# A fused attention and bilinear-FFN kernel whose whole order is written out as a table: one table of order, engines and PSUM banks is replaced by another

## The chip, the cores and the metric

The kernel runs on one core of a Trainium2 chip. The metric is device time in microseconds, the median of the timed runs. The kernel before takes 294.14 us (three runs: 294.15, 293.53, 294.14).

## The reference

Inputs are float32. Attention works in chunks of 64 tokens, each chunk for itself; its output goes through a bilinear feed-forward network.

```python
# q, k, v: (B=8, H=8, S=576, D=64);  w_a, w_b: (512, 1536);  w_out: (1536, 512)
scores = scale * q_c @ k_c.T              # per chunk of 64 tokens and head
attn   = exp(scores - max);  attn /= attn.sum(-1) + 1e-9
x      = (attn @ v_c) as (4608 tokens, 512)
a, b   = x @ w_a, x @ w_b
out    = ((a * b) @ w_out).astype(float32)    # (4608, 512)
```

## The kernel before, in words

**Tiling.** The 4608 tokens are nine blocks (K) of 512 tokens, and eighteen units (u) of 256 tokens; two units make a block. For each unit the kernel loads q, k and v (float32, by head), casts them to bf16 (`f32` to `qkb` and `vb`), transposes q and k into `qkT` (on TensorE for the first four units, `turn_pair`; with a transposing DMA from the SP queue after that, `turn_dma`), and then runs three short TensorE stages, called slots: scores into PSUM and exp on ScalarE into `E`; row sums through a matmul with `ones`, whose inverse is made by Ln and Exp(-x) on ScalarE (`inv`); values, multiplied by `inv` on VectorE into `xT`. These slots use 64x64 tiles of the array, all other matmuls the whole of it.

**FFN.** Block 0 is done plainly (`ffn`, L772): for each of twelve groups `ft` of 128 columns of the hidden layer one product with `WB` and one with `WA` (four matmuls of 512 columns each; for the first four groups each product is cut in two halves, so that it can start on half of the input), a copy of the first out of PSUM (`bsb`) and a multiplication (`AB`). From block 1 on the products are done by a seven-product scheme (`side_group`, L861; output: `out_seven`, L1166; last output block: `out_last`, L1004) on sums and differences of inputs (`x_sums`, `SX`), of weights (`side_sums`, `weight_sums`) and of `AB` (`out_sums`), made on VectorE or GpSimd. Each product is 4 or 6 matmuls of 256 columns; partial results are copied out of PSUM between products that share a bank (`keep_copy`).

**Loads.** Weights come as float32 in pieces of 512 KB into a ring of eight buffers (`wst`): `load_four` for WB and WA, `load_wo` for WO; each is cast to bf16 by one of GpSimd, ScalarE and VectorE. Nearly all loads and stores go through the SP queue, in the order of the table.

**Order.** Nothing is scheduled at run time. Every piece of work is an operation with a number, recorded by `Planner.op` with its dependencies. `Planner.follow` then reads the table `ORDER_OF_ALL`. A word is a letter for the engine that runs it (a TensorE, b ScalarE, c VectorE, d GpSimd, e the SP queue), the operation's number, and for an operation that takes PSUM banks their numbers. So `a49:0` is operation 49 on TensorE in bank 0, and `c50` is operation 50 on VectorE. `f0` is a fill: a matmul of zeros into bank 0, 512 columns wide, whose result nobody reads (L1474). Operations without a choice of engine keep theirs; casts, copies and sums may stand under one of two or three engines.

```python
for word in table.split():
    if word[0] == "f":
        order.append(fill(int(word[1:])))       # a matmul of zeros
        continue
    name, _, banks = word[1:].partition(":")
    o, e = self.ops[int(name)], self.ENGINES[word[0]]
    assert e in o["engs"] and o["deps"] <= done
```

**A wait that the table makes.** When an operation of VectorE that reads and writes SBUF alone (`fast`) stands in the table, the next GpSimd operation in the table gets a dependency on it.

**Operations that the text below names.** 48, 51, 57, 60, 66, 69, 75, 78: casts of the first block's q and k. 84, 85: casts of its v. 94, 95: reciprocals of row sums (VectorE). 13, 15, 17, 19: casts of the first pieces of WB and WA. 91, 92, 97, 98: the first four multiplications into `xT`. 32, 34 (loads) and 33, 35 (casts): the last pieces of WA. 118, 119, 137, 138 (loads) and 132, 151 (casts): v of units 2 and 3. 208, 227; 220, 271; 224, 275: the scores, sums and values slots of units 2 and 3. 225, 226, 276, 277: their multiplications into `xT`. 287, 289, 351: first products of block 1. 268, 269 (casts), 270 (transposing DMA) and 308 (scores): unit 5.

Of the kernel before, what the change touches and what calls it, by code (L numbers as in the profile page):

```python
# [97 lines left out]
a341:6 c207 a336 b337 d251 d255 d257 d286 e44 e38 a338 b339 d39 e263 b45 c199 a331:7 c332 c203 a342 a340:3  # L98
b343 a382:5 a351:1 a345 c344 e42 e262 e40 d41 b346 c347 a349:7 b350 a353 b354 a362:2 c363 a355 a359 c360 a357
c358 b43 a364:0 a372:2 b352 c365 a369 d268 e46 c230 a367 b47 c238 c242 a411:6 b370 a376 c377 c378 b368 a373  # L100
d231 d243 c356 e265 e264 b269 a412 b374 a371:3 c375 a384 b413 b385 c233 c232 c239 c241 c234 c244 c240 e214
b383 e213 b218 a423:0 a390 a424 c391 e211 e212 b217 d335 a388 c389 a393:4 a380:7 b381 a426 a427 e216 b428 a400
a398 a431 a395:2 a386 b401 a432 a407 c237 e266 e267 b279 c236 a429:3 d235 c425 b433 c394 c387 e270 b399
a308:04 b310 c396 b408 b309 a404 a430 a443 a320:12 b405 b321 a416 b322 d366 c348 a444 a414 c245 c361 c259 c261
c397 c434 c379 c453 a324:40 c445 e219 a280:12 b323 c325 a446 a447 c326 c448 a402:6 c406 b281 b282 a300:41 b302
b301 b303 e215 d278 a304:20 d435 c392 e292 e312 e291 a403:3 c409 d410 a418 c419 d457 c305 c306 a535:1 a420
c421 c436 c438 b415 b297 a526:4 a587:6 a536 a441:7 b442 a439:2 b440 a519:0 c520 d437 a524 b525 c417 e293 e294
d298 a517:3 a522 b523 c518 a531 b532 a527:0 c533 b537 a528 b529 c530 e311 a561:5 b562 b317 a579:3 a540 a544
a538 c545 c580 a584 c539 a542 c543 c541 e449 e314 e313 b318 a559:0 d422 d463 d521 b585 a577:3 a591 d459 c461
b560 c578 a582 b583 b592 c593 a597:2 c598 d454 d462 d534 d458 a612:4 a586:7 a588 b589 c590 d594 a595:3 b596  # L110
a605 c606 a599 c600 a619 e315 a601 a603 c604 c602 d456 d464 e465 e296 e467 a617 a614:6 a547:0 a548 b618 d455
b620 e316 b327 e299 a328:75 a623 a626 b330 b329 c615 a550 b627 e472 e319 a488:65 b489 b490 e466 c613 c624
a480:47 b482 c549 a638 c639 a640 c641 a551 c552 e295 d546 a622:0 b481 b483 a506:65 a510:37 b508 d307 a484:42
a555 c628 d616 e493 c486 c485 a621:5 c625 c629 c460 b507 e451 e498 e496 e468 a553:2 e494 e469 e452 e501 e471
b509 c512 c511 c630 c631 a753:6 a644 a693:4 a556 b557 e470 a636:7 a642 c643 e495 b477 e492 c645 d575 a554
a634:3 b637 a563 c632 d607 e474 a698 a564 b699 c635 a696 b565 c694 c558 c697 a691:5 a705 d646 c581 c692 d573
c574 a700:0 a701:4 a702 a566 a733:1 b706 c707 b478 b703 a712 e491 e450 b503 e497 b504 a567 c704 e500 a735:5
d633 a718 a716 b713 d608 e475 e476 e502 e473 c568 b487 a709:2 a760:3 c736 a758 c754 c719 b759 a710 b711 d647
d648 d650 a751:6 d609 c717 a714 c734 a756 c752 b757 c715 c720 a761:4 a765 b766 c767 a769:0 a762 a721:6 a771:7
a722 c763 a773 c764 a777 e499 e652 c723 d610 e651 e479 b772 b657 a779 a775 b774 c778 a793 b770 a791 e505  # L120
a668:61 d755 c780 c794 b670 a514:34 a724 a725 a800 b516 b515 a660:14 d768 d708 d611 c649 c792 c776 d781 c695
b669 a680:36 b681 b661 b682 b662 c726 e571 a788:5 c789 a797 b801 a786:3 a729 c787 c798 d513 a664:15 a684:64
b683 c685 c686 a730 b663 a814 a796:3 a812 a795:6 a727:4 a728 e572 e656 e672 e671 b677 c665 c666 a810:1 a825:5
d804 c805 e674 b731 b813 e673 e653 b678 c802 b811 a808:0 a818 c799 d576 d803 a737 a832 a738 a816 e654 b658
c809 c826 c790 c819 d782 c815 c817 c820 c806 a902:5 a830 e570 b739 e655 b833 a827:3 c828 a834:2 a835:7 b831
a836 b837 c732 a839 c840 c841 e676 e675 b687 a900:6 c838 d807 a846 a740 d749 c747 d748 b903 a925:3 a852 c853
a850 c851 a932 b901 a930 c926 c933 d667 d784 b931 b847 a741 c742 a848 c849 a936 a934:7 b937 c938 e679 a865:23
b870 e659 e858 a688:04 b689 b690 a947 c783 d829 c948 a939 e855 a927:1 c928 c940 a935:3 c941 a864:04 d750 b869
a892:62 b896 b895 a951 a943:1 c952 e885 e884 e882 c944 b867 b866 b868 a945:2 a843:6 c946 a949 c950 a844 a953
c954 b845 a962:4 d821 d889 c963 c822 a970:7 a967 c968 a891:05 a914:34 c929 b897 c917 c823 d942 e886 c916 c893  # L130
c978 a965 b966 a874 a875 b876 e887 b920 e856 a960:4 a974 e883 b888 c975 c976 c894 d842 c961 e857 b862 a969:3
a871:0 a872 a879 a971 b972 c973 a984:5 a880 a992 a986 c985 d955 d854 d979 a877:4 a1006 a878 c987 e569 e745
c873 b861 e860 d980 a990 e859 e1059 c993 c991 e746 c1007 a982:1 b983 d981 d898 a1074:0 c824 a1001:7 c1002
a1004 a988 a999:3 c1000 b881 d785 a904 a1008:7 b1005 a1010 a905 a1009:3 b1011 c956 e744 a1013 b1014 c899 a907
a1020 a908 d964 c989 c977 c994 c995 d957 a1103:2 c1012 a1024 d996 b1021 c1015 a1026 c1075 c1104 b906 a1076:1
b1077 d921 c1025 a1108 a1105:6 b1109 a1110 c1027 b1111 c909 a1022 c1023 e890 a1039:27 b1044 c1106 e1030 e1031
e743 e863 a915:34 b918 b1043 b919 a1114 c1115 a1112:5 c1116 a1117 c1118 a1121:7 a1066:63 b1070 b1069 c1122
a1038:24 b1040 a1125 c1126 b1041 b1042 a1129 e1029 e1034 d998 e1032 c1130 e1056 d923 d922 d1003 a1138:3 c1139
e1057 e1058 e1060 c1036 a1127 a1113:6 c1128 a1092:20 b1035 c1016 a1065:45 c1067 a1017:3 a1143 a1123:1 a1018
a1045:4 c1119 b1071 c1095 c1124 c1094 d1062 b1019 b1144 a1131 a1140:0 e912 c1132 a1149 a1046 c1150 e1033 e910  # L140
e1210 e1061 e1235 b1072 e1209 a1048 a1049 b1050 e913 a1147:2 a1145 b1146 c1068 a1164 c1047 c1141 d959 d958
d1156 d997 a1053 e1208 c1157 e1212 c1107 c1159 c1158 c1120 b1063 a1054 b1055 c1165 a1152 b1153 a1148:6 c1154
a1160:5 a1051:4 a1162:0 c1151 b1161 d1028 d924 a1170 c1171 a1168 c1169 a1179:7 a1182 a1078 a1079 a1177:6 a1052
b1163 c1183 a1252:2 a1184 b1185 c1180 c1133 d1142 c1178 d1181 d1155 a1188 c1189 a1186:7 b1080 a1187:6 a1166
a1277:3 a1191 c1073 a1081 a1082 d1136 c1190 c1167 d1172 d1175 b1253 a1254:1 a1202 d1099 d1134 c1192 c1193
a1204 a1200 d1194 e1037 e1064 d1100 b1255 a1282 c1203 b1283 c1278 c1083 c1205 a1198 b1199 c1201 a1284 c1285
a1288 b1289 a1286:7 c1290 a1217:34 a1093:56 b1096 b1221 a1279:0 c1280 b1222 a1291 b1292 a1295:5 a1299 d1206
# [1378 lines left out]
```

## Time and profile before

| | |
|---|---|
| Median of the timed runs | 294.14 us |
| Span of the profiled execution | 291.4 us |
| Median less span | 2.7 us |
| TensorE (PE) busy | 285.0 us, 98% of the span, 3522 matmuls |
| VectorE (DVE) busy | 245.6 us, 84% |
| ScalarE (ACT) busy | 181.5 us, 62% |
| GpSimd (POOL) busy | 175.3 us, 60% |
| HBM | 37.75 MB read, 9.44 MB written |

The profile gives the profiled execution's span, from its first instruction to its last, and no other time of that execution; the row below the span is the distance to the median. PE is the matmuls, PEld the loads of stationary operands, SPq the SP queue's own instructions. A matmul's length in the profile runs to its modelled end, and the next one starts before that: the distance between the starts is what a matmul costs TensorE.

### The profile page before, as it was taken

To read this page: it belongs to the slowest core of one execution; us is meant where nothing else is said; L and a number is where in the kernel's file an instruction comes from. 1 tells how busy PE (TensorE), PEld (TensorE's weight loads), DVE (VectorE), ACT (ScalarE), POOL (GpSimd) and SP (SyncE) were. 2 spreads that over 40 slices of the span, in tenths; PEclk is the share of its full clock that TensorE was granted. 3 is DMA by queue.
4 is the path that set the end of the run, shared out by engine and by line. 5 is a ranking of instruction groups with operands and counts; after the bars stand their busy time and mean duration, and the time that the engine had idled before them with its cause. 6 is when DMAs were issued, how large, how long until landed. Compare 5 with 4: busy or idle time off the path is not lost.

```text
span 291.4 us, 8635 instructions
## 1 busy us (share of the span) xinstructions
PE 285.0 (98%) x3522; PEld 232.6 (80%) x3522; DVE 245.6 (84%) x432; ACT 181.5 (62%) x308; POOL 175.3 (60%) x168
## 2 busy tenths in 40 slices
PE   8999989999999999999999999999999999999995
PEld 3545448887888888888888888888888888888884
DVE  2758989999897999989998989888997788697893
ACT  1767878978877775795675468525944684333221
POOL 3354248443789389835739694569447764676540
PEclk9999999999999999999999999999999999999999
DMA  7999999999998789939996995939290210003034
GB/s 244 335 395 393 310 282 340 246 216 246 213 213 219 191 175 274 240 75 201 260 259 158 203 277 126 253 88 242 76 219 3 80 69 2 0 2 144 3 133 156
DMA packets 140248, 55.09 MB, mean 189 GB/s; under 512 B 126256, under 2 KB 131504, under 8 KB 140208
## 3 DMA queue, kind: packets, MB, share of 16 engines
q1 hardware_dynamic: 138976, 53.43, 71.8%
q10 hardware_dynamic: 1232, 1.11, 1.1%
q8 instruction: 27, 0.44, 0.7%
q14 instruction: 13, 0.11, 0.1%
HBM read 37.75 MB, written 9.44 MB: 162 GB/s over the span
## 4 chain that ended last, share of the span: by engine, by line
PE 91%; ACT 3%; DVE 2%; DMA 1%; issue 1%; POOL 0%; SPq 0%; POOLq 0%
PE F L861 49%; PE F L1166 24%; PE F L772 6%; PE F L1004 3%; PE F L1474 2%; PE F L635 1%; PE F L645 1%; PE F L492 1%; PE F L673 1%; DMA f<-in_k_dram 1%; ACT inv L697 1%; ACT inv L695 1%; DVE xT L722 0%; POOL wst L821 0%; ACT E L528 0%
## 5 line engine op out<-in xcount | busy, mean ns | idle before, releaser
L326 ACT COPY part<-F 128x512 f32<-128x512 f32 x87 | 50.4, 591 | 49.0 <-PE F L861 32.2
L895 POOL TENSOR_TENSOR AB<-AB,bsb 128x512 bf16<-128x512 bf16 x45 | 51.7, 1156 | 38.7 <-DVE wst L1123 15.5
L899 DVE TENSOR_TENSOR bsb<-F,part 128x512 bf16<-128x512 f32 x72 | 49.0, 685 | 10.4 <-PE F L861 4.9
L326 ACT COPY wst<-F 128x512 f32<-128x512 f32 (+1 forms) x43 | 24.0, 561 | 30.5 <-PE F L861 14.7
L861 PEld LDWEIGHTS <-WB 128*128 128x128 bf16 x384 | 37.3, 98 | 5.2 <-issue 0.5
L861 PEld LDWEIGHTS <-WA 128*128 128x128 bf16 x384 | 37.2, 98 | 4.8 <-issue 0.3
L899 DVE TENSOR_TENSOR AB<-F,part 128x512 bf16<-128x512 f32 x48 | 32.9, 686 | 3.7 <-PE F L861 1.6
L1123 POOL TENSOR_TENSOR wst<-AB 128x512 bf16<-128x512 bf16 x27 | 31.0, 1155 | 7.0 <-PE F L1166 4.7
L861 PEld LDWEIGHTS <-Ta 128*128 128x128 bf16 x288 | 27.9, 98 | 3.9 <-issue 0.5
L861 PEld LDWEIGHTS <-Tb 128*128 128x128 bf16 x288 | 27.4, 98 | 4.4 <-issue 0.9
L1166 PEld LDWEIGHTS <-AB 128*128 128x128 bf16 x288 | 28.0, 98 | 3.4
L1166 PEld LDWEIGHTS <-wst 128*128 128x128 bf16 x288 | 27.8, 98 | 3.4
L861 PE MATMUL F<-wst,Ta 128*128 128x256 bf16 x192 | 28.8, 273 | 0.1
L861 PE MATMUL F<-wst,Tb 128*128 128x256 bf16 x192 | 28.8, 273 | 0.0
L861 PE MATMUL F<-wst,WB 128*128 128x256 bf16 x192 | 28.8, 273 | 0.0
L861 PE MATMUL F<-wst,WA 128*128 128x256 bf16 x192 | 28.8, 273 | 0.0
L861 PE MATMUL F<-xT,WA 128*128 128x256 bf16 x192 | 28.2, 273 | 0.0
L861 PE MATMUL F<-xT,WB 128*128 128x256 bf16 x192 | 28.1, 273 | 0.0
L1166 PE MATMUL F<-WO,AB 128*128 128x256 bf16 x192 | 25.5, 273 | 0.0
L326 DVE COPY part<-F 128x512 f32<-128x512 f32 x33 | 22.4, 684 | 2.7 <-PE F L861 2.0
L326 ACT CAST qkb<-f 128x1024 bf16<-128x1024 f32 (+1 forms) x24 | 23.2, 986 | 0.3 <-DMA f<-in_q_dram 0.3
L1123 POOL TENSOR_TENSOR wst<-wst,AB 128x512 bf16<-128x512 bf16 x16 | 18.4, 1155 | 6.0 <-DVE wst L1123 5.9
(126 smaller groups left out, 551.7 us busy)
## 6 DMA issues: line engine op xcount, KB each, us to landing
f<-in_q_dram SPq DMA_DIRECT2D x32, 256.0 KB, 4.2
f<-in_v_dram SPq DMA_DIRECT2D x32, 256.0 KB, 4.2
f<-in_k_dram SPq DMA_DIRECT2D x28, 256.0 KB, 4.8
out_dram<-osb SPq DMA_DIRECT2D x28, 256.0 KB, 3.5
wst<-in_moe_w_b_dram SPq DMA_DIRECT2D x6, 512.0 KB, 7.8
wst<-in_moe_w_a_dram SPq DMA_DIRECT2D x6, 512.0 KB, 6.9
wst<-in_moe_w_out_dram SPq DMA_DIRECT2D x6, 512.0 KB, 6.8
out_dram<-osb SPq DMA_DIRECT2D x12, 128.0 KB, 2.4
```

The lines of the kernel that those rows point to most:

```text
L326: return A.copy(out=out, in_=in_) if e == "act" else ENG[e].tensor_copy(out=out, in_=in_)
L492: T.transpose(turned()[:, r, :], qkb[hu][:, x, mm * 512 + r * 128:mm * 512 + r * 128 + 128], identity)
L635: T.matmul(PS[j][cl * 64:cl * 64 + 64, c:c + 64], chunk_of(u, 1, m, j, 2 * g + cl), chunk_of(u, 0, m, j, 2 * g + cl), start=True, stop=True,)
L645: T.matmul(SU[cl][j * 64:j * 64 + 64, :], ones[cl * 64:cl * 64 + 64, :], E[u % 2][cl * 64:cl * 64 + 64, j, :], start=True, stop=True,)
L772: T.matmul(f_of(b)[:, 0:n].rearrange("p (u t) -> p u t", u=len(us)), w[ft][:, kt, :], x[:, us[0]:us[-1] + 1, kt, :], start=(kt == 0), stop ...
L861: T.matmul(f_of(bank)[:, q * 256:q * 256 + 256], lhs(2 * g + q, kt), rhs[:, kt, :], start=(first and q == 0 and kt == 0), stop=(q == 1 and ...
L895: op(("dve", "pool"), TIMES, lambda e: ENG[e].tensor_tensor(out=dst, in0=dst, in1=b, op=MULT), r=bk, w=key, prio=-300, fast=True)
L899: op("dve", c_dve(512), lambda e: V.tensor_tensor(out=dst, in0=two(f_of(bank)), in1=two(pab[s][i]), op=ADD), r=[("ps", id(bank)), ("part", ...
L1004: T.matmul(f_of(bank)[:, 0:256], lhs[:, i, h], rhs[:, i, :], start=(first and i == 0), stop=(i == NP - 1), skip_group_check=True)
L1123: op(*long_op(hs), lambda e, i=i, x=x, y=y, o_=o_: ENG[e].tensor_tensor(out=SS[i][:, s], in0=x[:, s], in1=y[:, s], op=o_), r=fts + [(name, ...
L1166: T.matmul(f_of(bank)[:, at:at + 256], lhs[:, i, tt * 128:tt * 128 + 128], rhs[:, i, :], start=(first and at == 0 and i == 0), stop=(i == ...
L1474: "fn": lambda e: T.matmul(F[at], zero[:, 0:128], zero, start=True, stop=True),
```

## The change

`ORDER_OF_ALL` is another table over the same 1675 operations; nothing else differs. No operation is added or dropped. Of the fills 22 are left of 30. Engine changes: 51 operations go from VectorE to GpSimd and 46 the other way, 43 from ScalarE to VectorE and 40 the other way, 11 from ScalarE to GpSimd and 10 the other way. TensorE has the same 578 operations in another order and in other banks; the SP queue has the same DMAs in another order.

Lines of the table that the text below speaks of (before is -, after is +):

```diff
-c113 e0 b1 e2 b3 e4 e8 b5 e6 e9 c48 f0 f1 f2 f3 f4 f5 f6 f7 f0 f1 a49:0 c50 d51 f2 a52:1 d57 f3 f4 a58:2 b7
-d60 e10 e11 f5 a61:3 d66 b62 c53 a54:45 c59 f6 f7 a63:67 e12 b55 b56 a67:0 c68 b64 b65 f1 f2 a93:12 d69 a70:3
-b71 f4 f5 f6 a72:45 c94 b73 a86:67 b74 b75 b88 d78 a79:0 b80 f3 f3 f4 a76:3 b77 f5 f1 f4 f5 a81:45 a99:17 b87
-c84 c95 d85 a96:03 c97 f6 a90:62 b89 c91 d13 e16 d17 e135 e14 d15 c98 e18 e134 e20 e22 b83 b101 b82 f5 a106:50
...
-b128 a204:4 e136 e24 d148 a149:6 b150 c122 c25 c258 e26 c27 c252 c247 c254 c256 b206 b202 a196:7 a208:03 b210
-b209 e137 a227:12 b228 b229 a181:6 c183 c198 a192:4 b194 a185:5 c187 e138 e32 a220:30 a271:12 a177:4 e34 d33
-c35 c179 a189:6 c191 d249 e119 e118 c132 a193:7 a205:5 c260 b222 d253 b151 a224:04 b221 b223 c225 c226 d285
-b273 b272 b274 a275:36 c276 e36 b37 a201:2 a197:1 c277 c283 c284 c195 a287:0 b288 a289:4 b290 a333:3 c334
...
+c113 e0 b1 d48 f0 f0 f0 f0 f0 f0 f0 a49:0 c50 e2 b3 e4 b5 d51 d57 a52:1 c53 f2 a58:2 e6 b7 d60 c59 f3 a61:3 b62 e9 b69
+f4 f4 f4 a63:45 b65 e11 a54:67 e8 c75 f0 a76:0 c78 c77 f1 a79:1 b64 a93:23 a70:5 c95 b55 b66 b56 b80 a86:46 b88 b87
+d84 c71 c94 a67:0 a81:71 b83 b82 a106:64 b68 b108 b107 f1 f1 a72:17 e10 d85 f3 f3 f3 f3 f3 a90:30 b74 b89 a110:54
+a96:67 c98 e12 c13 e16 d17 e14 d15 b73 a99:12 b100 c91 c97 a103:71 c92 a152:3 b109 c111 b101 c112 b102 c104 a164:2
...
+b120 a121:4 c150 b147 b131 a189:2 b122 a208:03 b194 e32 a227:64 a196:7 b210 b209 c183 a220:13 b228 b229 a177:0 d33 e34
+c260 c258 c191 c198 d35 a197:2 c253 a271:64 c179 d255 a193:7 a205:0 b221 b222 b223 b273 e137 c187 e138 d151 b272 c199
+e118 e119 c132 a224:13 c195 c226 c225 d285 a275:52 e36 e44 e265 e263 b274 c277 c276 c283 c284 a201:4 b37 c257 a351:6
...
```

More of the change, by code (lines that the diff above doesn't have):

```diff
@@ new lines @@
+a1267:06 b1387 e1263 a1374 e1264 d1276 d1368 c1379 d1355 d1380 b1270 b1386 a1435 b1436 a1437:4 c1441 a1446:3 b1447
+b1271 a1450 c1375 c1451 a1442 a1454 c1455 a1468 a1400:07 b1403 d1432 a1381:26 b1384 c1443 c1275 a1438:1 c1444 d1347
+d1348 b1469 a1463:4 a1448:0 c1464 a1465:6 c1449 c1466 d1445 d1467 b1383 a1474 b1475 b1404 a1456 a1452 c1453 c1457
+b1385 a1369:4 c1458 a1489 b1490 a1399:26 a1421:75 c1402 b1405 c1422 a1370 b1371 c1423 a1470 b1471 a1472:1 a1388:3
+a1477 b1478 d1350 a1473:6 a1389 c1476 a1493 c1479 a1391 c1401 a1487:7 a1485:5 d1483 c1488 a1491 c1492 a1392 c1480
@@ new lines @@
+d1519 b1581 a1602 d1579 a1597:5 b1583 c1600 c1598 a1520:2 b1603 a1521 b1522 a1604 a1606:7 a1608 a1539 c1605 a1532:6
+a1628:4 a1611 b1612 a1535 a1533 c1609 c1501 a1615 c1592 a1536 d1566 d1593 d1594 d1558 a1630:5 a1631 c1534 a1617
+a1607:6 c1613 c1610 d1559 e1419 e1420 b1537 b1616 c1618 a1540 a1541 a1629 c1560 e1418 a1632:0 e1417 b1542 c1543 a1621
+a1619 a1548 a1549 b1550 a1638 c1601 a1634:1 a1635 a1633 b1639 a1636 b1637 d1614 a1551 a1552 e1555 e1554 c1622 c1620
+c1623 c1624 a1648:6 a1643 c1625 c1595 c1553 e1556 e1557 a1646 b1647 c1626 c1627 c1596 c1644 e1645 a1640 c1641 e1642
@@ L175 @@
+a1649 b1650 a1652 b1653 c1654 e1655 a1656 b1657 a1651:2 c1658 e1659 a1660 c1661 b1662 e1663 d1561 a1664 c1665 e1666
+a1670 b1673 b1674 c1671 e1672 a1667 c1668 e1669
 """
```

145 lines of the change are left out of this document (64 added, 81 removed).

## The prediction, made before the changed kernel was run

> **What bounds the kernel now.** I read the profile's page first, then the busy time by stretches, then the chain that ended last, then the waits of TensorE before and after 43 us. From the page, the busy times:
>
> ```profile
> PE 285.0 (98%) x3522; PEld 232.6 (80%) x3522; DVE 245.6 (84%) x432; ACT 181.5 (62%) x308; POOL 175.3 (60%) x168
> ```
>
> From the stretches (us; busy PE, PEld, DVE, ACT, POOL; granted clock; DMA share; GB/s), and from the chain and the waits after 43 us:
>
> ```profile
> 30.00:40.00 10.00, 9.17 (x111) 3.95 (x109) 8.52 (x15) 9.19 (x17) 2.25 (x3) 1.00 0.95 283
> 240.00:260.00 20.00, 20.00 (x186) 17.86 (x184) 15.69 (x29) 7.22 (x13) 11.32 (x11) 1.00 0.00 1
> 252.80 5.24 PE F L861 x48
> PEld L635 <- DMA f<-in_k_dram: 0.2, 1, 0.2
> ```
>
> From block 1 on (43 us) TensorE is the limit: 48 matmuls of 256 columns take 5.24 us, 109 ns each, and the longest wait for data in that stretch is 0.2 us. A new order can't make that part shorter; it can only break it. What can be won lies before 43 us, where TensorE idles and the DMA engines are full (share about 1), so the sum is made over three things: when the FFN starts, what TensorE has to do after that, and where it waits. It is made against the profiled execution, whose span is 291.4 us; the median of the runs is 294.14, 2.7 above it, and I carry the 2.7 over unchanged.
>
> **Start of the FFN.** The timeline of the head:
>
> ```profile
> 3.37 2.34 PE L1474 MATMUL F<-zero 128*128 128x512 bf16 x5
> 9.39 0.69 DVE L326 COPY qkT<-F 128x512 bf16<-128x512 bf16 x1 [1.11 <-PE F L492]
> 10.09 1.76 DVE L551 RECIPROCAL inv<-F 128x256 f32<-128x256 f32 x1
> 12.46 1.04 POOL L326 CAST vb<-f 128x1024 bf16<-128x1024 f32 x1 [3.31 <-DVE vb L326]
> 12.89 1.03 PE L1474 MATMUL F<-zero 128*128 128x512 bf16 x4
> 14.14 0.31 PE L570 MATMUL F<-E,vb 64*64 64x64 bf16 x16
> 14.38 1.04 POOL L326 CAST WB<-wst 128x1024 bf16<-128x1024 f32 x1 [0.88 <-DMA wst<-in_moe_w_b_dram]
> 14.58 1.64 DVE L583 TENSOR_TENSOR xT<-F,inv 128x256 bf16<-128x256 f32 x4 [0.53 <-ACT inv L555]
> 16.28 1.46 PE L772 MATMUL F<-xT,WB 128*128 128x512 bf16 x6
> ```
>
> Before, the FFN starts at 16.28, right after four multiplications into `xT` on VectorE (14.58 to 16.22); the cast of the first WB (operation 13) ran on GpSimd and was over at 15.42. After, VectorE gets, in this order: reciprocal 95, a copy out of PSUM (71), reciprocal 94, multiplication 98, cast 13, multiplications 91, 97, 92. The last v load is the twelfth in both orders, so operation 85 ends near 13.5 as before; behind it TensorE runs the values products, which the table puts behind five fills (0.22 us each by the 12.89 row: four take 1.03 with the end), near 14.05; 0.44 us later (14.14 to 14.58 before) VectorE can start 98, at 14.5. The two reciprocals and the copy take 1.76 + 0.69 + 1.76 from about 9.9, so VectorE is free at 14.1. Four multiplications (1.64) and the cast, now VectorE's (0.69, as in the row of 37.93 below), give 16.8: +0.5 on 16.28; less, if they follow each other more closely than before. ScalarE has new work ahead of the fifth fill (the casts 69 and 66 and the copy 68): I find that its queue would run 0.6 us later if matmuls still started 0.43 us apart, as in the first row, until about 9 us, which gives +1.1. I take +0.5, with +0.2 to +1.3.
>
> **What TensorE has to do after that.** Its operations are the same; one fill (f4 before operation 127) falls into the FFN, +0.2. Each change between 64x64 slots and full matmuls costs time:
>
> ```profile
> 65.70 0.82 PE L1166 MATMUL F<-wst,AB 128*128 128x256 bf16 x6
> 66.44 0.41 PE L645 MATMUL F<-E,ones 64*64 64x512 bf16 x4
> 66.79 0.61 PE L861 MATMUL F<-xT,Ta 128*128 128x256 bf16 x4
> 121.51 0.60 PE L861 MATMUL F<-wst,Ta 128*128 128x256 bf16 x4
> 122.04 0.63 PE L645 MATMUL F<-E,ones 64*64 64x512 bf16 x8
> 122.60 0.61 PE L861 MATMUL F<-xT,WA 128*128 128x256 bf16 x4
> ```
>
> A single sums slot costs 66.79 - (65.70 + 6 x 0.109) = 0.44 us, two in a row 122.60 - (121.51 + 4 x 0.109) = 0.65. In the old table the slots stand in 25 stretches, in the new one in 27 (220 and 271 are apart, and so is a values slot of units 6 and 7): 2 x 0.22, +0.45.
>
> **Stalls that go.** The timeline from 36 us, and the longer pieces of FFN work in the chain:
>
> ```profile
> 22.39 4.75 PE F L772 x22
> 36.18 1.67 PE L772 MATMUL F<-xT,WA 128*128 128x512 bf16 x7
> 37.93 0.69 DVE L326 CAST WA<-wst 128x1024 bf16<-128x1024 f32 x1 [1.18 <-DMA wst<-in_moe_w_a_dram]
> 38.69 1.47 PE L772 MATMUL F<-xT,WA 128*128 128x512 bf16 x6 [0.83 <-DVE WA L326]
> 39.74 0.74 DVE L326 CAST vb<-f 128x1024 bf16<-128x1024 f32 x1
> 40.54 0.73 PE L660 MATMUL F<-E,vb 64*64 64x64 bf16 x64 [0.38 <-DVE vb L326]
> PEld L492 <- POOL qkb L326: 0.7, 2, 0.5
> ```
>
> 4.75 / 22 = 0.216 us for a matmul of 512 columns. Seven from 36.18 are done at 37.69, the next starts at 38.69: 1.00 us lost to the last piece of WA. Six more are done at 39.99, values start at 40.54: 0.55, of which 0.1 is the change of tile: 0.45 lost to v. Two transposes lost some 0.4. Together 1.85. In the new table they go, if the loads come in time:
>
> ```profile
> 24.75 3.86 SPq L355 DMA_DIRECT2D f<-in_v_dram  x2
> 28.66 3.66 SPq L355 DMA_DIRECT2D wst<-in_moe_w_a_dram  x2
> 32.00:33.00 1.00, 1.00 (x47) 0.60 (x33) 0.97 (x2) 1.00 (x3) 0.00 (x0) 1.00 0.54 129
> 34.00:35.00 1.00, 1.00 (x9) 0.33 (x10) 0.96 (x3) 0.88 (x2) 0.00 (x0) 1.00 1.09 412
> ```
>
> Before, two v loads (137, 138) stood ahead of WA's last two pieces (32, 34) in the SP queue; their issue held the queue to 28.61 and WA's to 32.3, and the transfers sank to 129 GB/s where 412 is their full rate. After, 32 and 34 stand ahead of all four v loads. At full rate the two (1 MB) take 2.5 us; two v loads fewer ahead of them (0.5 MB, 1.3 us) and no hole put WA's landing at 34 to 36 instead of 37.9, and TensorE needs it near 37 (20.3 us of work after the FFN's start). The last v load is the last of the first 36 loads either way, so v lands no later than before, by 39.7; the values slot 224 comes after 23.5 us of TensorE work (15 products of 0.864, 16 halves of 0.432, eight transposes of 0.22, four slots, the fill) from a start at 16.8, at 40.3, and its cast needs 0.8 of that: just covered. So -1.85; if the holes return, -1.0.
>
> A second stall, 0.3 us, stands at 77.97, and its cause was a sum on GpSimd behind VectorE's:
>
> ```profile
> 76.76 1.15 POOL L821 TENSOR_TENSOR wst<-xT 128x512 bf16<-128x512 bf16 x1 [1.54 <-DVE wst L821]
> 77.97 0.31 PEld L861 LDWEIGHTS <-Ta 128*128 128x128 bf16 x3 [0.26 <-issue]
> ```
>
> In the new table that sum (437) stands some two us earlier against its product: -0.3, at least 0.
>
> **Waits that are new.** At the border of blocks 0 and 1:
>
> ```profile
> 41.10 2.48 DVE L714 TENSOR_TENSOR xT<-F,inv 128x512 bf16<-128x512 f32 x4
> 41.21 1.90 PE L772 MATMUL F<-xT,WA 128*128 128x512 bf16 x8
> 42.94 0.49 PE L861 MATMUL F<-xT,WB 128*128 128x256 bf16 x3
> ```
>
> Multiplications follow each other at 0.6 us, so the two that the first product of block 1 reads are ready 1.4 us after the first values slot. Before, the second slot (0.3) and eight matmuls (1.73) covered that; after, one product of four (0.86) does: 1.15, short by 0.25. Behind the waiting product stand all of block 1's. Further on VectorE's queue is a little denser than before, but two queues' sums taken side by side leave no other product more than 0.25 us short up to the end: +0.25, with 0 to +0.8. For the moved engines I book nothing: VectorE's 84% and the others' 60% still lie beside TensorE; where that cover fails, it is this term that grows. The order of the last products and stores is the same.
>
> Then the transposing DMA of unit 5 (270):
>
> ```profile
> 56.72 5.77 SPq L603 DMA_TRANSPOSE qkT<-qkb  x2
> 64.22 0.45 PE L635 MATMUL F<-qkT 64*64 64x64 bf16 x32
> qkT<-qkb SPq DMA_TRANSPOSE x14, 4.1
> 53.29 1.08 ACT L326 CAST qkb<-f 128x1024 bf16<-128x1024 f32 x1
> ```
>
> Its scores (308) come 43.7 us of work after the FFN's start, at about 60.5 instead of 64.22. The cast 269 ends 1.6 us (a copy and itself, 0.5 + 1.08) after a product that stands 5.5 us ahead of 308; with the median 4.1 from issue to landing that makes 5.7. 270 is also moved past two v loads of the SP queue (216 and 267), which now wait behind it, with a cast of v (279) behind those that has 2 us to spare. +0.1, with 0 to +2.
>
> **The sum.** +0.5 + 0.2 + 0.45 - 1.85 - 0.3 + 0.25 + 0.1 = -0.65. I forecast a span of 290.75 and a time of 293.5 us.
>
> **Rivals.** First, the head stays slow. The first row of the head shows 0.43 us a fill, 12.89's shows 0.22: in this run TensorE worked at half rate from 1.26 to about 6.7, with ten fills in an unbroken row. The new table has seven, which end at 4.3, and then gaps that no fill covers. If half rate returns by the FFN's start and lasts as long again (5.4 us), 2.7 us are lost: -0.65 + 2.7 gives 296.2; half of that, 294.8. It decides from the point where matmuls at 17 us start 0.43 apart. Against it: in the slow state the same operations keep TensorE busy for longer, and from 5 to 9 us hardly a gap is left. The Trainium skill, "TensorE: Matmul & The Clock Gate", Part 1, says that the array runs at half clock until a busy window of about 3.4 us has passed and falls back after an idle one; by that rule seven fills (3.0 us) fill no window, but no gap I find reaches 3.4 us either. Chance 0.14.
>
> Second, 270 lands no earlier than before, near 62.5 (the end of the 56.72 row), because the queue ahead of it is no shorter in time: 308 waits 2 us, 295.4. For it: the issue of the two transposes took 5.77 us. Against it: two loads fewer ahead. Chance 0.10.
>
> Third, the loads' holes return elsewhere and only half of the 1.85 goes: 294.4. Chance 0.14. Fourth, the head is no later than before and the border waits for nothing: 292.7. Chance 0.12. My forecast's own case, 292.9 to 293.9, has 0.50.
>
> **How the numbers follow.** About 0.2%, 0.59 us, is what a measurement of this kernel can tell. Faster means below 293.55: the fourth case and 0.34 of the first, 0.46. Same: 0.16 of the first and 0.11 of the third, 0.27. Slower (over 294.73): the slow head, the late transpose and the rest of the third, 0.27. The range, 292.5 to 295.5, leaves out the upper half of the slow head, part of the late transpose and a little below; the likeliest case's own is 292.9 to 293.9.
>
> **What would show it.** Right: the first L772 matmul between 16.5 and 17.6; no wait of L772 for a cast of WA; the first L861 matmul 0.3 to 1.0 us before 42.94; from there to the end as long as before, within 0.6 us. Wrong: matmuls at 0.43 us after 15 us; L635 waiting for `qkT` near 61; waits of L861 for VectorE or GpSimd of over 1 us in sum after 45 us.

## The result, and the profile after

The changed kernel takes 295.3 us (294.2 to 296.5, ten runs) against 293.97 us of the kernel before (293.47 to 294.48, ten runs beside it): ratio 1.0048, 95% interval 1.0033 to 1.0063. It is 1.3 us slower where the prediction said 0.65 faster. The forecast's direction was wrong; its range (292.5 to 295.5) held the median by 0.2 us.

Each run's time lies 1.8 us above its span. So the profile of the kernel before (span 291.4) is of an execution of about 293.2 us, quicker than any of its ten runs, and that of the changed kernel (span 294.7) of its slowest, 296.5: the 3.3 us between the spans are 2.0 more than the medians differ by, and the 2.7 us that the prediction carried over are the 1.8 and 0.9 between executions. Of these 3.3 us the traces give this account; the two rows of the middle are differences of the starts and ends around them:

| | before | after | difference | predicted |
|---|---|---|---|---|
| first FFN matmul starts | 16.28 | 16.94 | +0.66 | +0.5 |
| from there to the first product of block 1 | 26.66 | 27.75 | +1.09 | -0.9 to -1.5 (42.0 to 42.6, less 16.8) |
| from there to the last matmul's end | 245.23 | 246.76 | +1.53 | within 0.6 |
| from there to the end | 3.21 | 3.26 | +0.05 | 0 |

**The head.** TensorE's rows in the timeline of the changed kernel (start, length, what ran, idle time before it and what ended it):

```profile
11.93 0.30 PE L535 MATMUL F<-E,ones 64*64 64x256 bf16 x4 [0.77 <-ACT E L522]
15.35 0.32 PE L564 MATMUL F<-E,vb 64*64 64x64 bf16 x16 [0.49 <-DVE xT L577]
16.94 2.50 PE L766 MATMUL F<-xT,WB 128*128 128x512 bf16 x6 [1.28 <-DVE xT L577]
19.24 2.14 PE L766 MATMUL F<-xT,WA 128*128 128x512 bf16 x6
```

Six matmuls of 512 columns take 2.30 us from the first start to the seventh's, 0.38 each, where the kernel before needed 0.216. The busy time by stretches says why (first number after the stretch's length: PE; third from the end: granted clock). The last row is of the kernel before:

```profile
10.00:17.00 7.00, 4.47 (x123) 2.42 (x121) 6.03 (x9) 5.92 (x16) 2.65 (x3) 1.00 1.04 329
16.00:18.00 2.00, 1.06 (x4) 0.42 (x5) 2.00 (x7) 0.71 (x2) 1.04 (x1) 0.80 1.03 393
18.00:20.00 2.00, 2.00 (x6) 0.69 (x5) 0.21 (x1) 0.00 (x0) 0.97 (x1) 0.50 1.05 406
20.00:22.00 2.00, 2.00 (x9) 0.88 (x8) 0.53 (x1) 0.15 (x1) 1.11 (x2) 0.85 1.06 390
10.00:17.00 7.00, 6.51 (x140) 3.56 (x137) 5.56 (x8) 5.68 (x16) 3.12 (x3) 1.00 1.10 353
```

After three idle spells that no fill covers, the granted clock falls to half just as the FFN begins: 0.80, 0.50 and 0.85 over three stretches of 2 us lose 2 x (0.20 + 0.50 + 0.15) = 1.7 us. In the kernel before TensorE was busy for 6.51 of the 7 us ahead of it, here for 4.47. Three of the ten runs have a mean clock of 0.992 to 0.994 (this one 0.992), the others 0.998 to 1.000. The three took 296.0 us on average and the other seven 294.9, which is still 1.0 us above the kernel before (293.9): the half clock is dear in the runs that have it, but most of the loss is there without it.

**The border of blocks 0 and 1.** The loads of v in SyncE's queue, the stretch behind them, and what TensorE then does:

```profile
29.33 7.41 SPq L349 DMA_DIRECT2D f<-in_v_dram  x4
36.00:39.00 3.00, 3.00 (x78) 1.41 (x77) 2.79 (x6) 2.89 (x7) 1.04 (x1) 1.00 0.86 192
42.02 0.69 DVE L320 CAST vb<-f 128x1024 bf16<-128x1024 f32 x1 [0.51 <-DMA f<-in_v_dram]
42.77 0.71 PE L654 MATMUL F<-E,vb 64*64 64x64 bf16 x64 [0.22 <-DVE vb L320]
44.69 0.72 PE L855 MATMUL F<-xT,WA 128*128 128x256 bf16 x5 [0.25 <-DVE xT L708]
```

The wait for WA is gone. But four v loads in a row hold the queue for 7.41 us, the transfers sink to 192 GB/s (386 to 397 from 24 to 34 us), and the last v lands at 41.92, against 39.58 in the kernel before. TensorE was late itself by the half clock, so that it lost 0.22 us to v.

**After block 1 has begun.** The cast that feeds the transposing DMA of unit 5, that DMA, and its scores; then the stretch around it, first before, then after; then the only waits for data in TensorE's list after 20 us (us in total, times, longest):

```profile
57.78 1.08 ACT L320 CAST qkb<-f 128x1024 bf16<-128x1024 f32 x1
58.90 3.64 SPq L597 DMA_TRANSPOSE qkT<-qkb  x1
63.11 0.60 PE L855 MATMUL F<-xT,Tb 128*128 128x256 bf16 x4
64.85 0.45 PE L629 MATMUL F<-qkT 64*64 64x64 bf16 x32 [1.14 <-DMA qkT<-qkb]
45.00:67.00 22.00, 22.00 (x231) 19.06 (x230) 21.53 (x41) 18.57 (x30) 12.83 (x12) 1.00 1.13 263
45.00:67.00 22.00, 20.73 (x218) 18.12 (x217) 21.39 (x41) 17.13 (x29) 10.67 (x10) 1.00 1.03 235
PE F L629 <- DMA qkT<-qkb: 1.1, 1, 1.1
PE F L855 <- DVE xT L708: 0.2, 1, 0.2
PE F L654 <- DVE vb L320: 0.2, 1, 0.2
```

270 is issued as soon as its cast is done and lands at 64.81, 5.9 us later; 308 waits 1.14 us. In a stretch in which TensorE never stopped before, it now idles for 1.27 us. After 70 us no matmul's wait for data is listed in either trace.

### The profile page after: what moved, and what is told of

It is laid out like the page before. It is cut to its first block, busy times and chain, and to the rows that moved or that the text cites. A ratio compares the mean times of both kernels' runs of the same rounds, so it can differ in the third digit from the quotient of the medians.

```text
span 294.7 us, 8628 instructions
## 1 busy us (share of the span) xinstructions
PE 285.5 (97%) x3514; PEld 232.4 (79%) x3514; DVE 248.5 (84%) x430; ACT 177.2 (60%) x304; POOL 184.1 (62%) x174
## 2 busy tenths in 40 slices
DMA packets 140248, 55.09 MB, mean 187 GB/s; under 512 B 126256, under 2 KB 131504, under 8 KB 140208
## 4 chain that ended last, share of the span: by engine, by line
PE 78%; DMA 14%; SPq 4%; DVE 2%; issue 1%; ACT 0%; ACTq 0%; DVEq 0%; POOLq 0%
PE F L855 46%; PE F L1160 24%; SPq L349 4%; DMA f<-in_k_dram 4%; DMA wst<-in_moe_w_a_dram 3%; PE F L998 3%; DMA wst<-in_moe_w_out_dram 2%; DMA f<-in_v_dram 2%; DMA qkT<-qkb 2%; PE F L629 2%; PE F L667 2%; PE F L639 1%; DVE AB L893 0%; DVE xT L708 0%; DVE AB L781 0%
## 5 line engine op out<-in xcount | busy, mean ns | idle before, releaser
L320 ACT COPY part<-F 128x512 f32<-128x512 f32 x84 | 48.4, 589 | 54.5 <-PE F L855 47.3
L889 POOL TENSOR_TENSOR AB<-AB,bsb 128x512 bf16<-128x512 bf16 x46 | 52.8, 1155 | 33.0 <-DVE wst L1117 6.3
L1117 POOL TENSOR_TENSOR wst<-AB 128x512 bf16<-128x512 bf16 x31 | 35.5, 1154 | 12.4 <-PE F L1160 3.6
L320 DVE COPY part<-F 128x512 f32<-128x512 f32 x36 | 24.7, 685 | 5.5 <-PE F L855 4.8
L1117 POOL TENSOR_TENSOR wst<-wst,AB 128x512 bf16<-128x512 bf16 x17 | 19.6, 1156 | 3.8 <-DVE wst L1117 2.0
L320 ACT CAST bsb<-F 128x512 bf16<-128x512 f32 x28 | 16.4, 591 | 9.1 <-PE F L766 6.4
```

What stands on the lines that cost most here:

```text
L320: return A.copy(out=out, in_=in_) if e == "act" else ENG[e].tensor_copy(out=out, in_=in_)
L889: op(("dve", "pool"), TIMES, lambda e: ENG[e].tensor_tensor(out=dst, in0=dst, in1=b, op=MULT), r=bk, w=key, prio=-300, fast=True)
L1117: op(*long_op(hs), lambda e, i=i, x=x, y=y, o_=o_: ENG[e].tensor_tensor(out=SS[i][:, s], in0=x[:, s], in1=y[:, s], op=o_), r=fts + [(name, ...
```

## The experiments

My theory after the result (A): two causes, the half clock that the gaps of the head bring on, and the late DMA 270 ahead of 308. Rival B: the later start and the moved engines cost the time, and what the trace shows as waits stands beside others that are as late. Every kernel below was timed in five rounds beside the kernel before; differences are medians against that kernel's runs on the same chip (293.55 to 293.98). The last column counts runs with a mean clock of 0.994 or less.

| kernel | difference, us | ratio, 95% interval | half clock |
|---|---|---|---|
| changed kernel | +1.3 | 1.0048 (1.0033 to 1.0063) | 3 of 10 |
| head_fills | +0.2 | 1.0011 (0.9992 to 1.0029) | 0 of 12 |
| scores_later | +1.7 | 1.0048 (1.0028 to 1.0069) | 3 of 9 |
| fills_and_scores | +0.8 | 1.0023 (1.0000 to 1.0047) | 0 of 12 |
| before_loads | -0.1 | 0.9997 (0.9978 to 1.0016) | 1 of 12 |
| fewer_fills | +2.4 | 1.0078 (1.0051 to 1.0105) | 6 of 6 |
| g13_only | +0.8 | 1.0031 (1.0011 to 1.0050) | 0 of 12 |
| g13_and_fills | -0.1 | 1.0000 (0.9981 to 1.0018) | 0 of 12 |
| g13_fills_v266 | +0.1 | 0.9990 (0.9973 to 1.0007) | 0 of 12 |
| g13_scores_later | +0.9 | 1.0027 (1.0012 to 1.0042) | 0 of 12 |
| g13_casts | +1.4 | 1.0058 (1.0035 to 1.0082) | 0 of 7 |
| g13_v_first | +1.6 | 1.0065 (1.0039 to 1.0091) | 1 of 6 |
| all_four | +1.9 | 1.0061 (1.0043 to 1.0079) | 0 of 6 |
| after_424 | +0.9 | 1.0035 (1.0015 to 1.0054) | 2 of 11 |
| g13_424 | +1.1 | 1.0035 (1.0013 to 1.0057) | 0 of 11 |
| best | +0.6 | 1.0012 (0.9994 to 1.0030) | 0 of 11 |
| g13_424_320 | +0.4 | 1.0020 (1.0000 to 1.0041) | 0 of 12 |
| best2 | +0.5 | 1.0020 (1.0006 to 1.0034) | 0 of 12 |

### More fills, and fewer

**head_fills**:

```diff
-b83 b82 a106:64 b68
+b83 b82 f6 f6 f6 a106:64 b68
-a99:12 b100 c91 c97 a103:71 c92 a152:3
+a99:12 b100 f7 f7 c91 c97 a103:71 f6 f6 f6 f6 f6 c92 a152:3
```

> The changed kernel with ten more fills on TensorE: three ahead of the sums of operation 106 (idle there 0.77 us), two ahead of 103 (0.49) and five ahead of the first FFN product (1.28). Theory A (two causes: a stretch at half clock that the gaps of the head bring on in some runs, and the late DMA 270): the granted clock shows no 0.50 between 16 and 22 us, matmuls of the FFN follow at 0.216 us from the first, the first starts near 16.9 as in the changed kernel; every run has clock 1.000, and the median is that of the changed kernel's seven runs with clock 0.998 or more, 294.9 (295.3 before); the wait of 308 for qkT stays, about 1.3 us. Rival B (the later head itself and the moved engines cost the time, the clock is chance): the median stays within 0.2 us of 295.3, and half-clock stretches come as often as without the fills. Rival C (the fills are in the way): the first FFN matmul comes later than 17.2, 295.6 or more.

Timeline and stretches of head_fills:

```profile
16.58 1.24 PE L1468 MATMUL F<-zero 128*128 128x512 bf16 x5 [0.42 <-DVE xT L577]
17.66 0.59 PE L766 MATMUL F<-xT,WB 128*128 128x512 bf16 x2
10.00:17.00 7.00, 5.79 (x132) 3.05 (x131) 6.21 (x10) 5.79 (x16) 2.08 (x2) 1.00 1.06 328
16.00:18.00 2.00, 1.58 (x23) 0.82 (x16) 2.00 (x7) 0.67 (x2) 0.95 (x1) 1.00 1.06 410
18.00:20.00 2.00, 2.00 (x11) 0.88 (x9) 0.18 (x1) 0.00 (x0) 1.67 (x3) 1.00 1.05 407
```

The bank of the last five fills was free only at 16.58, so that the fills put the FFN back to 17.66, 0.72 later than in the changed kernel; that much of rival C came true. And yet this kernel is 1.1 us nearer to the kernel before, and 1.5 us below scores_later (below), which ran on the same chip with the changed kernel's head. No run of the twelve fell to half clock.

**fewer_fills**:

```diff
-f1 f1 a72:17
+a72:17
-d85 f3 f3 f3 f3 f3 a90:30
+d85 a90:30
```

> The changed kernel without the two fills ahead of 72 and the five ahead of 90, which stand beside a wait for v in any case. By theory A (the gaps in TensorE's work bring the half clock on) the half clock comes in every run and no later than 17 us, clock 0.994 or less, and lasts as long or longer: 1 to 2 us above the changed kernel, ratio to the kernel before 1.008 to 1.012. Rival B (fills have nothing to do with it): ratio 1.005 as with the changed kernel, clock 1.000 in over half of the runs.

Its busy time by stretches:

```profile
10.00:17.00 7.00, 3.21 (x124) 2.07 (x122) 6.19 (x9) 5.92 (x16) 2.08 (x2) 0.97 0.99 311
16.00:18.00 2.00, 0.72 (x8) 0.35 (x3) 2.00 (x7) 1.08 (x3) 0.40 (x1) 0.64 1.05 405
18.00:20.00 2.00, 2.00 (x6) 0.73 (x5) 0.58 (x2) 0.00 (x0) 1.68 (x2) 0.51 1.04 405
```

All six runs have a mean clock of 0.987 to 0.993, and the kernel is 2.4 us slower than the kernel before. Fills in, the half clock goes from all runs; fills out, it comes in all. In the traces of head_fills, the changed kernel and fewer_fills TensorE was busy for 5.79, 4.47 and 3.21 us of the seven from 10 to 17 us, with 0 of 12, 3 of 10 and 6 of 6 runs at half clock. That gaps in the head bring on the half clock is shown; that the clock is all that the fills change is not (see g13_and_fills below).

The seven microseconds are too long a measure, though: g13_casts (below) is busy for 4.48 of them, as the changed kernel is, and none of its runs fell. The traces have a better one. In each of the three that show the half clock (the changed kernel, scores_later and fewer_fills) it lasts 3.41 us. The least that TensorE was busy in any stretch of 3.41 us that begins between 4.5 and 17.5 us is 1.65, 1.65 and 0.94 us there, and 1.73 to 2.97 in the fifteen other traces that are read here. The stretch of least work and the one at half clock in the changed kernel, then the least of fewer_fills and of g13_424_320:

```profile
13.53:16.94 3.41, 1.65 (x72) 0.95 (x70) 2.44 (x7) 2.52 (x6) 1.16 (x2) 1.00 1.01 372
17.20:20.61 3.41, 3.41 (x10) 1.18 (x9) 1.01 (x4) 0.00 (x0) 1.66 (x3) 0.50 1.05 404
13.31:16.72 3.41, 0.94 (x60) 0.75 (x61) 2.67 (x5) 2.56 (x8) 1.04 (x1) 0.97 1.02 375
13.28:16.69 3.41, 1.73 (x72) 0.90 (x71) 2.69 (x7) 2.65 (x7) 1.76 (x2) 1.00 0.99 369
```

So TensorE idled for about half of such a stretch or more wherever the clock fell. Where exactly the line lies no run tests: best2 (below) has a stretch of 1.68 us behind its wait for v, and its clock did not fall. Two runs with a mean clock of 0.994 or less, one of before_loads and one of g13_v_first, have no trace. In the three traces the record of the granted clock begins at 6.96, 4.19 and 6.31 us, and the fall comes 10.24, 13.66 and 10.24 us later, which is three, four and three times 3.41. That looks as if the clock were settled at marks 3.41 us apart that lie differently in every execution, and would make it chance which runs of one order fall; it is read from three traces and not tested.

The Trainium skill, "TensorE: Matmul & The Clock Gate", Part 1, has the array fall back to half clock after an idle window of about 3.4 us; the longest gap here is 1.28 us, so that the trace doesn't bear that out as a condition. It agrees rather with the same page's section on a second failure mode, which tells of a kernel that cycles through PSUM banks and in which frequent short idling between groups of matmuls was enough.

### Operation 13 and the start of the FFN

**g13_only** (`c98 e12 d13` in place of `c98 e12 c13`):

> The changed kernel with one part undone: the cast of the first WB (operation 13) goes back from VectorE to GpSimd; no fill is added. It takes 0.69 us out of VectorE's row ahead of the FFN, so that the first FFN matmul starts near 16.3 in place of 16.94 and TensorE idles 0.6 us ahead of it in place of 1.28. If the half clock is brought on by how much TensorE idles between 11 and 17 us, the stretch at half clock goes from most runs, and the time is 0.65 + 1.0 lower, ratio to the kernel before 0.999 (1.005 for the changed kernel). Rival (only the start counts, the half clock comes by chance or by another gap): 0.65 lower, ratio 1.0025, half clock in as many runs as in the changed kernel.

The FFN began at 16.07, no run fell to half clock, and the ratio was 1.0031: the clock as theory A had it, the time nearer to the rival's 1.0025 than to 0.999. In its trace (span 292.8) the scores 308 wait for 270 as in the changed kernel:

```profile
62.82 0.45 PE L629 MATMUL F<-qkT 64*64 64x64 bf16 x32 [1.33 <-DMA qkT<-qkb]
```

Block 1 began at 42.76, 0.18 earlier than in the kernel before, but from there to the last matmul's end it takes 246.75 us, as in the changed kernel (246.76) and 1.5 more than in the kernel before (245.23). The start of the FFN is less steady than one trace shows: with operation 13 on GpSimd and no fill added, it lies between 16.07 and 16.77 in six traces, and with the changed kernel's head at 16.94 and 17.13 in two.

**g13_and_fills** (g13_only, with `f6 f6 f6` ahead of `a106` and `f3 f3` behind `a103:71`) and **g13_fills_v266** (the same, `e266` moved from ahead of `e214` to behind `e270`):

> Operation 13 back on GpSimd, three fills ahead of 106 and two in the gap behind 103, whose bank is free when the second multiplication into xT is done. With the ten fills alone the FFN began at 17.66, because the bank of the last five came free only at 16.56; here it should begin at 16.3, with no half clock after it. If start and clock are what the head costs, this is 1.3 us below the kernel with ten fills: ratio to the kernel before 0.9965, spans near 290.6. Rival (the loads decide when the first block ends, whatever the FFN's start): the stalls on WA and on v come back with about 1 us, ratio 1.000.

> As the kernel with operation 13 on GpSimd and five fills, with the v load 266 behind the transposing DMA 270 in SyncE's queue in place of three places ahead of it. If 270 is late because the eight transfers in flight ahead of it are still landing (issue 58.9 to 62.5, landed 64.8 in the changed kernel, 5.9 us), it lands about 1 us earlier against its scores 308, and the wait of 308 (0.3 to 1.2 us) goes: up to 0.5 us below its neighbour without this edit. Rival (270 waits for its cast on ScalarE, and the transfer takes its time whatever is ahead): no difference within 0.2 us.

Both are as fast as the kernel before (1.0000 and 0.9990). Fills are worth about 0.9 us here too (g13_only on the same chip stands at 1.0031), and here not by the clock, which fell in no run of either. The traces part at 308, which in g13_and_fills doesn't wait:

```profile
62.10 0.45 PE L629 MATMUL F<-qkT 64*64 64x64 bf16 x32
```

Block 1 begins at 43.42 with fills, 0.66 later than in g13_only, and 308 comes 0.72 earlier, because 270 landed 4.4 us after its issue and not 5.8. In the three traces with fills added to the head that have its landing (head_fills, fills_and_scores, g13_and_fills) it took 4.0 to 4.8 us, in the eight of the new order without them 5.2 to 5.9. Why is open.

The FFN's start at 16.27 in g13_and_fills gave little beyond that (head_fills, which began at 17.66, stands at +0.2): from there to block 1 it took 27.15 us, with gaps (start to start, less a matmul) of 0.27, 0.51 and 0.55 us at products and transposes that waited for their casts, of which the two of WB had waited for loads. The rival's time holds, and its reason in part: the waits stand at WB and at q and k, and not, as it said, at WA and v. With 266 out of the way 270 was issued in 1.68 us in place of 2.37, and 308 waited in neither trace, so that this question stayed open here. The eight transfers in flight of this expectation are not in the trace: in the changed kernel three loads were still to land when 270 was issued, at 59.74, 60.62 and 62.96.

**before_loads** (the kernel before, `e32 e34` ahead of `e137`) shows the same on the other side:

> The kernel before, with one part of the change alone: the last two pieces of WA's weights (loads 32 and 34) stand ahead of the two v loads 137 and 138 in SyncE's queue. If the stall of 1.00 us at 38.7 was due to that order, and the v loads then land as early as in the changed kernel (the last by 41.9): the 1.00 goes, the values slot at 40.5 waits for its cast of v about 1 us in its place or less: 293.0 to 293.6 against 294.0 of the kernel before. Rival (the loads fill their time in any order, so that v is later by as much as WA is earlier): the wait moves whole to the values slot, 294.0 within 0.3. Second rival (the block behind takes the gain back through its transposing DMA): a wait of 0.5 us or more for qkT appears near 64 us.

Busy time from 16 to 43 us, the kernel before and before_loads:

```profile
16.00:43.00 27.00, 25.71 (x293) 12.37 (x281) 21.23 (x37) 20.72 (x36) 10.66 (x13) 1.00 1.01 344
16.00:43.00 27.00, 26.69 (x307) 13.13 (x307) 21.80 (x38) 20.87 (x37) 11.63 (x13) 1.00 1.05 357
```

TensorE idles 1.0 us less in block 0, the waits for WA and v are gone from its list, and the median is 0.1 us lower, with an interval from 0.65 us less to 0.47 more. The profiled spans, 291.2 and 291.4, agree with that: block 1 began 0.7 earlier, and 308 0.16 earlier. So most of a stall that goes in block 0 is lost again by the scores 308.

**g13_v_first** (`e137 e138` back ahead of `e32 e34`, on g13_only):

> Operation 13 on GpSimd, and the other order of loads undone: the v loads 137 and 138 stand ahead of 32 and 34 in SyncE's queue again, as in the kernel before. If that order brought the 1.00 us wait of the FFN on the last piece of WA, it comes back near 38 us, and the last v load lands 0.5 to 1 us earlier; the first product of block 1 comes 0.5 to 1.0 later than in g13_only (42.76). As 270 holds 308 up to 62.8 in any case, the time would move by 0.3 or less (ratio 1.003 to 1.005) if theory A is right that gains ahead of 308 end at its wait; a full 1.0 us (1.006) if not.

No wait for WA came back: the cast 35 ended at 38.34, and in this table TensorE doesn't need it before. So the order of the loads alone didn't take that wait away; the place of the products that read WA's last piece did its part. v landed at 39.13 in place of 39.98. The ratio, 1.0065, is higher than either theory said; six runs on another chip don't settle why.

### The scores 308

**scores_later** and **fills_and_scores** (the latter with the ten fills), and **g13_scores_later** (on g13_only):

```diff
-a308:24 b309 b310 b408 a426 a427 a403:2 b415 b428 a418 a424 c425
+b408 a426 a427 a308:24 b415 b428 b309 b310 a424 a418 a403:2 c425
```

> The changed kernel with the products 426 and 427 (16 matmuls of 256 columns, 1.74 us) ahead of the scores 308 in place of behind them, and 424 and 418 ahead of 403. Theory A: the wait of 308 for the transposed qkT (1.1 us, the gap of 1.31 at 64.85) goes and nothing takes its place: 294.1 (1.2 less than 295.3), half-clock stretches in a part of the runs as before. Rival B (a wait that only hides another, further on the scores 320 and 280 of the neighbouring slots or VectorE's queue are as late): half or none of it, 294.7 to 295.3, with a new wait of over 0.5 us at 320, 324 or 280.

> Both edits together, the ten fills of the head and the later scores 308. Theory A: the two gains add, 0.4 and 1.2, 293.6 to 293.8, that is as fast as the kernel before or a little faster, every run at clock 1.000. Rival B: no faster than 294.6.

> The kernel with operation 13 on GpSimd, in whose trace 308 waited longest for the transposed qkT (a gap of 1.50 us at 62.82), with 426 and 427 ahead of 308 as in the run scores_later. Theory A (270's landing decides as soon as the head is quick): the wait goes, some 0.5 us of it comes back at 426, which waits for VectorE: 0.9 below g13_only, ratio to the kernel before 1.000. Rival B (the body takes it back elsewhere): 1.003 as g13_only.

From the timeline of scores_later:

```profile
63.67 1.48 PE L1160 MATMUL F<-TS,wst 128*128 128x256 bf16 x12 [0.35 <-DVE wst L1117]
65.08 0.45 PE L629 MATMUL F<-qkT 64*64 64x64 bf16 x32
```

The wait of 308 is gone, and the product that went ahead of it waits for VectorE's sum instead. The medians don't move: 1.0048 as the changed kernel, 1.0023 with fills (without the edit 1.0011), 1.0027 against 1.0031. So the second half of theory A is not borne out: with the wait of 308 gone the time is what it was, as rival B says. fills_and_scores is 0.9 us below scores_later, so the fills show again.

**g13_casts** (268 and 269 on GpSimd and a little earlier, `e38 d268 d39` and `e264 d269 c233`; 266 behind 270) and **all_four** (g13_and_fills, these casts, 266, and `a220:13` moved to just ahead of `a271:64`):

> Operation 13 on GpSimd, and the transposing DMA 270 itself made earlier: its two casts 268 and 269 go from ScalarE to GpSimd, which idles around 55 and 57 us, and the v load 266 stands behind 270. 270 should be issued at 55.5 to 57 in place of 57 to 58.9, and land by 61.5 to 62; 308 then waits 0.3 or nothing in place of 1.4. Theory A: 1.1 below g13_only, ratio to the kernel before 0.999. Rival (the transfer takes the place that the loads leave it, whatever its issue): it lands at 62.5 or later and the ratio stays 1.003.

> Operation 13 on GpSimd, five fills in the gaps of the head, the casts of 270 on GpSimd with 266 behind it, and the sums 220 and 271 side by side again, which saves one change of tile (0.22 us). If the causes are the half clock, the wait of 308 and the changes of tile, nothing is left but the loads: 0.5 to 1.0 us below the kernel before, ratio 0.997 to 0.998. Rival (the loads of the head decide, and what is won ahead of them is lost at them): 1.000, with waits of the FFN for casts of 0.5 us each.

Both came out slower. From g13_casts:

```profile
55.16 1.25 DVE L1117 TENSOR_TENSOR wst<-AB 128x512 bf16<-128x512 bf16 x1
57.18 1.26 DVE L1117 TENSOR_TENSOR spare_sum<-AB,wst 128x512 bf16<-128x512 bf16 x1
59.09 1.10 PE L1160 MATMUL F<-WO,AB 128*128 128x256 bf16 x6 [1.08 <-DVE bsb L893]
63.40 0.45 PE L629 MATMUL F<-qkT 64*64 64x64 bf16 x32
```

My edit broke something that the table took care of. These sums take VectorE 0.42 us elsewhere in this trace and in the changed kernel's; beside the casts on GpSimd (55.09 to 56.14 and 57.05 to 58.16) they take 1.25. VectorE fell 1.7 us behind, TensorE waited 1.08 for it, and 270, whose cast ended at 58.16 (56.92 in g13_only), landed at 63.35. So these two tell nothing of 270, except that with a clear queue (issue 58.19 to 59.87) it took 5.2 us to land all the same.

**after_424**, **g13_424** (`a424` moved to just ahead of `a308:24`, in the changed kernel and in g13_only) and **g13_424_320** (also `a320:47` ahead of `a431`):

> The changed kernel with one product half, 424 (8 matmuls of 256 columns, 0.87 us), ahead of the scores 308 in place of 4 places behind them; its inputs are those of 423, done before. Theory A: where 308 waits 1.2 us for 270, 0.87 of it is filled: 0.5 to 0.9 below the changed kernel, ratio to the kernel before 1.002 to 1.003. Rival B (the wait of 308 stands beside another that is as late): 1.005, and a new wait at 426, 431 or 320 of 0.5 us or more.

> The same with operation 13 on GpSimd, where the head is quicker and 308 waited 1.4 us. Theory A: the whole 0.87 is won, ratio to the kernel before 1.000 in place of 1.003. Rival B: 1.003.

> Operation 13 on GpSimd, 424 ahead of 308, and the sums slot 320 ahead of 431 in place of behind it, which fills the 0.35 us in which 431 waited for ScalarE's copy 428. Theory A (the wait of 308 is a price of its own): 308 waits 0.6 in place of 1.4 and nothing new waits after it: 0.4 below the kernel with 424 alone, ratio to the kernel before 1.002. Rival B (VectorE and the loads are as late as 270): a new wait of 0.4 us further on, ratio 1.0035.

after_424 has no trace that could be read beside the others. The first two rows are of g13_424, the others of g13_424_320:

```profile
63.04 0.45 PE L629 MATMUL F<-qkT 64*64 64x64 bf16 x32 [0.56 <-DMA qkT<-qkb]
66.13 0.82 PE L1160 MATMUL F<-wst,wst 128*128 128x256 bf16 x6 [0.35 <-ACT wst L320]
62.50 0.45 PE L629 MATMUL F<-qkT 64*64 64x64 bf16 x32 [0.17 <-DMA qkT<-qkb]
65.59 1.47 PE L1160 MATMUL F<-wst,wst 128*128 128x256 bf16 x12
```

424 had covered a copy of ScalarE; with 320 in its place both waits are nearly gone. The ratios are 1.0035 for after_424 (1.0048 without the edit), between theory and rival; 1.0035 for g13_424 (1.0031 without), as rival B says; and 1.0020 for g13_424_320, as theory A says. All three differences are well inside the intervals. The traces show the wait; that it costs the time is not shown.

### Versions with the edits left standing

**best**: g13_and_fills, 266 behind 270, 220 beside 271, 424 ahead of 308. **best2**: best, `a320:47` ahead of `a431`, `c226 c225` ahead of `c195`.

> Operation 13 on GpSimd, five fills in the gaps of the head, 266 behind 270, the sums 220 and 271 side by side, and 424 ahead of 308; the casts of 270 stay on ScalarE. With the fills and 266 the ratio to the kernel before was 0.999; 220 and 271 together save 0.2 us and 424 up to 0.9 where 308 would wait. Theory A: ratio 0.996 to 0.998, the span near 291. Rival (the loads of the head decide): 0.999 to 1.000.

> As best, with 320 ahead of 431 (0.35 us idle there) and, at the border of blocks 0 and 1, the two multiplications 226 and 225 ahead of the copy 195 on VectorE, so that the first product of block 1 waits 0.4 us less. Theory A: 0.7 below best, ratio to the kernel before 0.998 to 0.999. Rival (what is won ahead of 62 us is lost at 270): 1.001.

Neither beats the kernel before. best's profiled run began block 1 at 42.10, just as the prediction had it (42.0 to 42.6), and best2's at 44.10, behind this wait:

```profile
41.43 0.69 DVE L320 CAST vb<-f 128x1024 bf16<-128x1024 f32 x1 [1.99 <-DMA f<-in_v_dram]
42.18 0.71 PE L654 MATMUL F<-E,vb 64*64 64x64 bf16 x64 [1.55 <-DVE vb L320]
```

The last v landed at 38.72 in the one and at 41.34 in the other, from issues at 34.4 and 34.8 under the same order of loads. In the other traces of the changed kernel's load order that have the landing it lies anywhere from 39.05 to 41.92.

## Why the prediction was wrong

**Start of the FFN**: +0.5 forecast, +0.66 measured. Right, and the engine that it named, VectorE with the cast 13, is what g13_only took away; the start then fell to 16.07, and to 16.11 to 16.77 in the other traces with that head.

**Stalls that go**: -1.85 forecast. The wait for WA went, for part of the reason given. The step that failed here is "v lands no later than before, by 39.7": it landed at 41.92, because the last v load was issued at 35.89, 3.0 us later than before, behind a hole in the loads like the one that two v loads had made. The half clock hid most of it in this trace; best2 has a wait of 1.55 us for v. Without the 1.7 us of the clock, the stretch from the FFN's start to block 1 is 0.6 us shorter than before, and not 0.9 to 1.5. Nor is such a stall won whole at the end, as the sum took it to be: before_loads idles 1.0 us less in block 0 and is 0.1 us faster, by its interval 0.65 at most.

**The clock**: the first rival, with a chance of 0.14 and "2.7 or half of that". It happened in 3 of 10 runs, from the point that the prediction named, for 3.4 us in place of the 5.4 assumed, at 1.7 us. What failed is the argument against it: it looked at the gaps from 5 to 9 us and at none from 10 to 17, where they are. All of the eight fills that the table drops were to be costed by what they cover, and I costed only the one that was added. By the runs with and without fills, the fills that the head lacks are worth 0.9 to 1.1 us, the larger part of the loss of 1.3. The half clock is about 0.3 of it on average (296.0 us in three runs of ten, 294.9 in the rest), so that runs at a mean clock near 1.000 gain from fills too. The traces of g13_only and g13_and_fills, a pair without half clock, have that gain at 308, through a quicker landing of 270; what makes it quicker is open, and so is this part of the cause.

**270**: +0.1 forecast, 1.14 measured in the trace; the second rival. The cast was in time (58.86, against 63.54 when TensorE was ready). The term that was mis-sized is the transfer: I took the median 4.1 of its group, where the row of the same transfer in the kernel before was quoted beside it, 5.77 us for it and the next to be issued; it had taken 6.0 to land there. It took 5.9. In the medians this wait doesn't show: without it scores_later is as slow as the changed kernel.

**The border** (+0.25) was 0.25, and the rest of block 1 on (+0.45 - 0.3) was about +0.4, the 1.53 of the table less 1.14. One more change of tile stands in that part, priced at 0.22; the rest is not located.

**Moved engines**, booked at nothing: g13_only is 0.5 us better than the changed kernel by the medians, with overlapping intervals.

So the clock and the transfer were in the text, on the side of the rivals, and the sum booked the one at nothing and the other at 0.1. That the range held the median all the same was luck, as it came of costs that the sum had not priced. The gain that the sum did hold, block 1 at 42.1, came about in best and still made nothing faster: from there to the last matmul's end best takes 246.34 us, 1.1 more than the kernel before.

## What to carry to other kernels

Count the fills or other work that keep TensorE busy ahead of a long stretch as part of that stretch: look at how much of every 3.4 us ahead of it TensorE is busy, and neither at single gaps nor at a mean over a longer time. Before two profiles are compared, place each among the runs of its kernel: here one was quicker than all ten runs and the other the slowest. Price a transfer by its own row, not by the median of its kind. A stall that an earlier stall hides is still there: before booking a gain at one, follow the next two things that come late (here v, then the transposing DMA, then VectorE's sums): before_loads took 1.0 us of idle time out of block 0, and its median moved by 0.1.

## What the runs showed that I had not expected

TensorE fell to half clock after gaps of 0.77, 0.49 and 1.28 us within six, and stayed there for 3.4 us of unbroken work; the least busy 3.41 us ahead held 1.65 us of work, and in no trace whose least held 1.73 or more did the clock fall. The first fills of each run, 0.43 us apart, stand under a granted clock of 1.00, so that this column shows the fall-back and not the slow start. A VectorE sum of 512 bf16 columns in SBUF took 1.25 us beside a GpSimd cast, and 0.42 without. The last v load, issued at 34.4 to 36.0 under the same order, took from 3.9 to 6.6 us to land.
